# One four-tile MLP job split into two, under a new written order of all queues: two layers of banded attention and GELU MLP on one core

## The chip, the cores and the metric

The kernel runs on one core of a Trainium2 chip. The core has five engines with a queue each: TensorE (PE in the profile, its weight loads PEld), VectorE (DVE), ScalarE (ACT), GpSimd (POOL) and SyncE (SP), which here issues all DMAs. Every engine works through its own queue in the order in which the instructions were written, and waits on counters (semaphores) for the others. The metric is the device time of one execution in microseconds; less is better.

## The reference

Two layers, each an attention block (A) and an MLP block (B), both with a layer norm ahead and a residual sum behind. Both layers use the same weights. S = 2048 tokens, D = 512, 32 heads of 16, a causal band of W = 256 keys, F = 1792, all inputs bfloat16.

```python
def _A_ref(x, wqkv, wo):
    B, S, D = x.shape
    H = 32; Dh = D // H; W = 256
    q, k, v = ...                       # x @ wqkv, cut into heads
    scores = jnp.einsum("bhqd,bhkd->bhqk", q, k) * (Dh ** -0.5)
    mask = (idx[:, None] - idx[None, :] >= 0) & (idx[:, None] - idx[None, :] < W)
    scores = jnp.where(mask[None, None], scores, -1e9)
    p = _softmax(scores, axis=-1)
    o = jnp.einsum("bhqk,bhkd->bhqd", p, v)
    return (...)(o, 0, 2, 1, 3).reshape(B, S, D) @ wo

def _B_ref(x, w1, b1, w2, b2):
    h = jnp.einsum("bsd,df->bsf", x, w1) + b1
    h = _gelu(h)
    return jnp.einsum("bsf,fd->bsd", h, w2) + b2

x = A_x
x = x + _A_ref(_layernorm(x, axis=-1), A_wqkv, A_wo)
x = x + _B_ref(_layernorm(x, axis=-1), B_w1, B_b1, B_w2, B_b2)
x = x + _A_ref(_layernorm(x, axis=-1), A_wqkv, A_wo)
x = x + _B_ref(_layernorm(x, axis=-1), B_w1, B_b1, B_w2, B_b2)
```

## The kernel before

**Tiles and blocks.** The 2048 tokens are 16 tiles of 128. Over both layers they are counted on: tiles 0 to 15 are layer 1, 16 to 31 layer 2. An attention block b (0 to 15) is two tiles, 2b and 2b+1; blocks 0 to 7 are layer 1. X holds the running sum for all 16 tiles in on-chip memory.

**What one block does.** `lnq` (layer norm, transposed copy of the normed tile into xnTA by DMA, Q) and `kv` (K and V) come first. Then `attention(b)` goes through ten visits (five in blocks 0 and 8, where no keys lie behind). A visit is one set of score matmuls (L741), 512 score columns for each of four row groups, into four of the eight PSUM banks, then two exps on ScalarE (L748, two banks each) into the ring E, then masks (L769, VectorE or GpSimd). After five visits, and after ten, a PV (L793) multiplies E with V: 128 small matmuls (64 where no keys lie behind) that fill two banks; VectorE transposes (L802), inverts the sums (L806), scales (L810, VectorE or GpSimd) and transposes back (L816). Then come the output projection and the residual sum (L842) and the second layer norm, whose transposed tiles go to xnTB.

**MLP jobs.** `mlp(J)` (L846) handles the tiles of job J of the list JOBS (L457), an entry being (first tile, number of tiles). W1 (L857) makes 14 column groups of 128, four matmuls each, as wide as the job has tokens: 512 columns for four tiles, 256 for two. For the first six groups VectorE adds the bias (L865) and ScalarE applies the GELU to two groups at once (L868); for the other eight ScalarE does both (L873). W2 (L883) is 14 matmuls of 512 columns for each tile; GpSimd prepares X plus the second bias (L881), VectorE makes the sum (L885), and in layer 2 a DMA stores it. A job of even number reads xnTB half 0, of odd number half 1 (`js`), and a two-tile job uses the half J % 2 of gT.

**Exp and GELU.** ScalarE loads a table when it goes from exps to GELUs, and again on the way back (ACT_TABLE_LOAD in the profile).

**The order.** The functions put nodes into a plan (`_Plan.add`, L371); `run` (L391) then takes them in the order of the list `_ORDER`, gives the nodes named in `_ALT` to their second engine (evacuations L581/L583 VectorE or ScalarE; masks, L810 and part of the layer norm VectorE or GpSimd), and takes PSUM banks from `_BANKS`. `_PV_SEQ` is the order of the 32 groups of matmuls in a PV. `_Sched.op` records each node in its engine's queue with the waits that its tiles need. All plain projections and MLP matmuls are recorded by line L640 and are told apart by their tiles: W_sb with xnTB is W1, W_sb with gT is W2.

In ScalarE's queue, the GELUs of the job of tiles 4 to 7 stand after six exps of block 5, and those of tiles 8 to 11 after sixteen of block 7.

Of the kernel before, what the change touches and what calls it, by code (L numbers as in the profile page):

```python
# [19 lines left out]
class _Sched:  # L20
# [147 lines left out]
    33, 34, 0, 4, 7, 14, 17, 1, 13, 22, 18, 19, 56, 37, 36, 46, 35, 3, 26, 8, 41, 15, 27, 57, 60, 9, 61, 58, 39, 16,  # L168
    2, 59, 62, 20, 64, 28, 63, 10, 30, 24, 65, 11, 106, 104, 25, 47, 40, 67, 107, 105, 108, 38, 49, 54, 66, 32, 48,
    21, 68, 23, 31, 29, 69, 5, 80, 81, 82, 109, 55, 42, 110, 113, 111, 112, 114, 6, 83, 70, 71, 72, 73, 115, 126, 127,  # L170
    128, 129, 84, 74, 152, 130, 194, 195, 116, 117, 118, 119, 120, 97, 98, 99, 100, 150, 366, 85, 196, 101, 103, 368,
    86, 87, 88, 153, 151, 154, 75, 76, 77, 198, 367, 89, 155, 156, 200, 78, 12, 90, 91, 92, 93, 102, 79, 199, 131,
    132, 94, 157, 96, 95, 202, 204, 322, 121, 122, 123, 197, 133, 134, 203, 369, 124, 125, 136, 201, 137, 138, 205,
    158, 159, 216, 217, 143, 144, 145, 146, 135, 324, 139, 140, 212, 325, 323, 147, 218, 326, 327, 207, 519, 328, 208,
    209, 141, 329, 219, 214, 170, 171, 172, 173, 213, 370, 43, 160, 161, 162, 163, 174, 372, 371, 210, 520, 215, 374,
    164, 521, 148, 149, 175, 176, 376, 177, 178, 330, 375, 165, 166, 167, 206, 379, 179, 377, 381, 168, 380, 331, 44,
    142, 211, 220, 221, 180, 181, 182, 45, 183, 378, 169, 384, 385, 337, 222, 223, 373, 224, 338, 339, 340, 386, 394,
    395, 382, 388, 184, 186, 230, 231, 232, 233, 225, 226, 341, 383, 227, 396, 234, 237, 398, 228, 229, 400, 387, 389,
    238, 235, 185, 397, 236, 239, 399, 290, 402, 187, 188, 189, 190, 240, 390, 403, 241, 242, 243, 342, 343, 344, 522,
    345, 346, 407, 404, 405, 406, 191, 332, 333, 409, 334, 335, 336, 347, 348, 408, 412, 413, 414, 349, 350, 351, 244,  # L180
    50, 51, 192, 523, 524, 359, 360, 361, 362, 410, 527, 352, 353, 354, 355, 401, 356, 363, 563, 564, 245, 259, 525,
    260, 416, 357, 246, 261, 641, 252, 253, 565, 255, 275, 276, 277, 256, 254, 358, 411, 415, 257, 247, 258, 248, 249,
    262, 263, 264, 193, 528, 526, 284, 278, 364, 285, 250, 281, 269, 279, 280, 642, 282, 283, 270, 265, 391, 392, 417,
    639, 418, 640, 643, 271, 251, 393, 52, 53, 272, 644, 647, 266, 267, 273, 287, 365, 288, 286, 268, 645, 274, 307,
    308, 419, 420, 309, 310, 311, 312, 567, 544, 545, 546, 421, 547, 289, 306, 568, 313, 314, 315, 316, 571, 317, 569,
    529, 570, 530, 318, 646, 422, 531, 532, 572, 319, 320, 423, 548, 321, 573, 648, 575, 576, 533, 424, 425, 577, 427,
    428, 578, 429, 430, 539, 426, 487, 540, 541, 542, 431, 291, 581, 583, 543, 580, 434, 292, 293, 435, 582, 432, 294,
    295, 296, 574, 591, 592, 534, 535, 536, 537, 433, 593, 556, 538, 579, 557, 558, 898, 559, 896, 560, 436, 659, 660,
    561, 437, 297, 661, 662, 584, 595, 438, 439, 594, 298, 299, 300, 585, 649, 650, 651, 596, 566, 440, 652, 597, 663,
    586, 653, 599, 600, 549, 441, 587, 550, 301, 302, 303, 304, 305, 601, 602, 604, 551, 552, 605, 445, 446, 449, 450,  # L190
    606, 553, 447, 609, 562, 475, 476, 899, 897, 900, 472, 473, 610, 451, 459, 460, 456, 611, 452, 654, 461, 901, 904,
    453, 457, 607, 458, 902, 462, 442, 443, 655, 656, 454, 444, 469, 470, 598, 466, 471, 657, 658, 484, 485, 603, 664,
    665, 477, 448, 463, 608, 588, 474, 455, 481, 905, 482, 483, 464, 486, 612, 467, 468, 488, 489, 613, 589, 590, 465,
    478, 479, 490, 491, 614, 615, 480, 503, 683, 684, 492, 493, 666, 667, 616, 685, 494, 495, 687, 688, 668, 496, 497,
    498, 499, 686, 500, 501, 691, 617, 618, 669, 689, 690, 670, 671, 672, 693, 692, 502, 903, 916, 917, 918, 919, 694,
    673, 695, 675, 696, 698, 920, 624, 625, 626, 697, 699, 627, 504, 674, 628, 631, 701, 702, 619, 620, 621, 622, 623,
    505, 506, 555, 629, 630, 703, 711, 632, 507, 713, 508, 700, 509, 510, 511, 512, 633, 715, 906, 907, 704, 712, 908,
    716, 1018, 1019, 513, 514, 717, 705, 719, 721, 720, 1016, 634, 635, 637, 1017, 515, 909, 516, 517, 718, 638, 706,
    518, 724, 676, 714, 910, 1020, 707, 1021, 677, 678, 679, 723, 708, 726, 725, 729, 730, 680, 682, 926, 927, 928,
    933, 731, 636, 722, 934, 935, 728, 709, 710, 727, 936, 940, 929, 921, 922, 733, 923, 732, 941, 924, 925, 734, 937,  # L200
    938, 930, 939, 942, 944, 1024, 1022, 1023, 943, 946, 739, 740, 735, 948, 736, 911, 945, 912, 913, 737, 738, 914,
    950, 1025, 947, 741, 742, 949, 952, 915, 953, 955, 681, 951, 744, 743, 749, 745, 554, 746, 747, 748, 751, 954,
    958, 959, 750, 752, 1036, 1037, 1038, 957, 753, 754, 1039, 1040, 960, 968, 969, 757, 758, 1026, 970, 1027, 1028,
    1029, 755, 756, 962, 961, 972, 974, 1030, 973, 956, 976, 1275, 963, 977, 978, 971, 981, 975, 983, 964, 965, 966,
    786, 787, 788, 789, 982, 790, 986, 988, 1273, 781, 782, 979, 783, 932, 1274, 784, 785, 770, 771, 980, 987, 984,
    772, 1060, 985, 1062, 773, 990, 774, 764, 1061, 765, 766, 775, 767, 776, 777, 778, 1064, 1066, 768, 989, 991, 779,
    1065, 1068, 992, 817, 1063, 832, 818, 819, 1070, 802, 803, 1069, 1067, 807, 808, 827, 828, 829, 967, 996, 820,
    821, 993, 994, 759, 760, 761, 809, 810, 811, 848, 762, 1001, 1002, 997, 995, 998, 763, 999, 797, 798, 830, 1003,
    1004, 780, 1071, 1276, 1000, 1277, 769, 1278, 812, 813, 814, 791, 831, 822, 815, 816, 804, 805, 1005, 1008, 799,
    1009, 792, 823, 793, 794, 1395, 806, 795, 800, 1031, 796, 1006, 1279, 824, 825, 833, 864, 1007, 1393, 1032, 1072,  # L210
    1033, 1010, 1011, 834, 801, 1034, 1396, 826, 1035, 931, 849, 850, 835, 836, 1014, 1012, 837, 1281, 1073, 1074,
    851, 838, 852, 839, 840, 1075, 1076, 1078, 1079, 1080, 853, 841, 842, 854, 1015, 1041, 1042, 1043, 1044, 1045,
    1077, 855, 1082, 843, 844, 845, 1088, 1089, 856, 857, 1282, 858, 859, 860, 1081, 846, 861, 862, 847, 1092, 1090,
    865, 1091, 1093, 863, 1094, 881, 882, 1083, 1013, 1096, 883, 880, 866, 867, 1097, 1084, 868, 884, 1098, 1101,
    1103, 1099, 1085, 1086, 1087, 885, 886, 1102, 887, 888, 889, 890, 891, 1106, 869, 870, 871, 1095, 1394, 1397, 872,
    873, 1280, 1108, 1398, 1401, 1107, 1399, 1109, 1105, 892, 1317, 1319, 893, 874, 875, 876, 877, 1104, 894, 1318,
    1110, 1321, 1322, 1100, 878, 879, 1298, 1299, 1300, 895, 1301, 1302, 1293, 1294, 1323, 1295, 1296, 1325, 1111,
    1320, 1327, 1326, 1328, 1297, 1330, 1332, 1324, 1335, 1112, 1331, 1113, 1114, 1115, 1288, 1121, 1122, 1289, 1290,
    1337, 1291, 1292, 1225, 1334, 1336, 1345, 1123, 1329, 1124, 1116, 1125, 1128, 1338, 1347, 1117, 1118, 1119, 1346,
    1303, 1349, 1350, 1333, 1304, 1305, 1306, 1120, 1046, 1047, 1048, 1049, 1351, 1126, 1129, 1127, 1130, 1307, 1353,  # L220
    1354, 1131, 1309, 1134, 1283, 1135, 1284, 1355, 1285, 1132, 1133, 1286, 1358, 1339, 1340, 1050, 1287, 1360, 1359,
    1352, 1348, 1363, 1364, 1356, 1053, 1341, 1310, 1311, 1650, 1312, 1313, 1357, 1054, 1362, 1365, 1366, 1367, 1437,
    1439, 1055, 1056, 1136, 1137, 1314, 1400, 1138, 1361, 1139, 1342, 1368, 1051, 1057, 1059, 1058, 1438, 1140, 1402,
    1441, 1343, 1369, 1443, 1147, 1163, 1344, 1148, 1149, 1209, 1370, 1440, 1150, 1442, 1371, 1158, 1159, 1151, 1160,
# [189 lines left out]
def bass_interleave_layers__sliding_block__dense_activation_gelu__prompt_kernel(  # L414
# [39 lines left out]
    NWARM = 18  # L454
    PG = 2
    NPRE = 6
    JOBS = [(0, 2), (2, 2), (4, 4), (8, 4), (12, 4), (16, 4), (20, 4), (24, 4), (28, 2), (30, 2)]  # L457
    JLAG = 0
    W1_CUTS = ((0, 6), (6, 10), (10, 14))
    W2_CUTS = ((0, 4), (4, 8), (8, 11), (11, 14))  # L460
# [496 lines left out]
```

## Time and profile before

| what | value |
|---|---|
| median of 3 runs | 454.34 us (454.14 to 455.18) |
| the profiled execution | 452.28 us |
| its span on the core | 450.4 us |
| granted TensorE clock | 1.00 |
| busy TensorE, ScalarE, VectorE, GpSimd | 424.1, 388.0, 362.3, 204.1 us |
| exps L748 | 300, 1035 ns mean |
| GELUs L873 + L868, table loads | 80 + 30, and 18 of 1283 ns |
| last exp of block 3, 4, 5, 6, 7 ends at | 104.7, 126.4, 159.2, 181.3, 214.1 us |
| first W1 matmul to last X sum of job 2 (tiles 4 to 7) | 123.5 to 163.2 us |

The profile shows one execution. A group line names the source line, the engine, the operation and the tiles, the count, the busy time and the mean of one, and the idle time of the engine just before. A matmul's duration holds its way through the array, which overlaps the next matmul: eighteen matmuls of 512 columns that last 0.38 us each take 4.06 us together.

### The profile page before, as it was taken

How to read it: one execution, taken by the hardware profiler on the slowest of the kernel's cores; microseconds unless marked ns; L12 is line 12 of the kernel's file. 1: busy time of each engine (PE TensorE's matmuls, PEld its weight loads, DVE VectorE, ACT ScalarE, POOL GpSimd, SP SyncE). 2: the span in 40 equal slices, each digit the busy share in tenths (PEclk: the TensorE clock that was granted, in tenths of full speed). 3: DMA queues.
4: the chain of work that ended last, by engine and by line, in shares of the span. 5: the costliest groups of instructions: out<-in, count | busy, mean ns of one | idle time of the engine just before them, and what ended most of it. 6: DMA issues, size and time to landing. Idle time of an engine off the chain costs nothing.

```text
span 450.4 us, 16887 instructions
## 1 busy us (share of the span) xinstructions
PE 424.1 (94%) x7579; PEld 230.3 (51%) x7579; DVE 362.3 (80%) x650; ACT 388.0 (86%) x459; POOL 204.1 (45%) x219
## 2 busy tenths in 40 slices
PE   8979899997689988999999999999999999999997
PEld 4545656643444454455445444546555554544663
DVE  6999787989887689987899789877798768765852
ACT  3999898998889898899998998899897999899732
POOL 4476562453464445732284816653436143334320
PEclk9999999999999999999999999999999999999999
DMA  8684811112200201211022021010322013202000
GB/s 242 192 201 52 221 30 39 26 33 54 53 3 5 44 4 32 52 32 36 4 50 45 0 56 27 15 36 15 75 48 53 2 34 53 63 1 68 21 23 25
DMA packets 47972, 23.25 MB, mean 52 GB/s; under 512 B 33180, under 2 KB 47900, under 8 KB 47900
## 3 DMA queue, kind: packets, MB, share of 16 engines
q1 hardware_dynamic: 47900, 22.17, 21.4%
q8 instruction: 60, 0.98, 1.0%
q14 instruction: 12, 0.10, 0.1%
HBM read 8.00 MB, written 2.10 MB: 22 GB/s over the span
## 4 chain that ended last, share of the span: by engine, by line
PE 73%; DVE 20%; ACT 3%; DMA 2%; issue 1%; POOL 0%; DVEq 0%; SPq 0%
PE ps L640 57%; PE ps L793 8%; PE ps L741 7%; DVE E L769 4%; DVE OD L802 3%; ACT E L748 3%; DVE stat L592 2%; DVE Nb L810 2%; DVE KT L674 2%; DMA xnTB<-xn 2%; DVE xn L614 2%; DVE OT L816 1%; DVE X L885 1%; DVE X L842 1%; DVE Rc L806 1%
## 5 line engine op out<-in xcount | busy, mean ns | idle before, releaser
L748 ACT ACTIVATE E<-ps 128x1024 bf16<-128x1024 f32 x300 | 284.2, 1035 | 34.1 <-PE ps L741 33.1
L769 POOL TENSOR_TENSOR E<-E,mask 128x512 bf16<-128x512 bf16 (+2 forms) x111 | 123.3, 1122 | 144.0 <-ACT E L748 143.9
L640 PE MATMUL ps<-W_sb,gT 128*128 128x512 bf16 x448 | 116.2, 380 | 0.0
L640 PE MATMUL ps<-xnTB,W_sb 128*128 128x512 bf16 (+1 forms) x560 | 109.8, 337 | 2.1 <-DMA xnTB<-xn 1.4
L640 PEld LDWEIGHTS ps<-xnTB,W_sb 128*128 128x128 bf16 x560 | 51.9, 98 | 43.7 <-issue 4.1
L640 PE MATMUL ps<-xnTA,Wqkv_sb 128*128 128x256 bf16 x512 | 70.0, 273 | 4.1 <-DMA xnTA<-xn 2.2
L769 DVE TENSOR_TENSOR E<-E,mask 128x512 bf16<-128x512 bf16 (+2 forms) x125 | 63.7, 536 | 7.1 <-ACT E L748 7.0
L741 PE MATMUL ps<-QT,KT 32*128 32x128 bf16 (+3 forms) x1920 | 60.3, 231 | 7.8 <-ACT E L748 2.4
L640 PEld LDWEIGHTS ps<-W_sb,gT 128*128 128x128 bf16 x448 | 39.8, 98 | 41.5 <-issue 4.4
L640 PEld LDWEIGHTS ps<-xnTA,Wqkv_sb 128*128 128x128 bf16 x512 | 46.9, 98 | 24.2 <-issue 6.2
L741 PEld LDWEIGHTS ps<-QT,KT 32*128 32x128 bf16 x1920 | 28.3, 92 | 57.1 <-ACT E L748 34.5
L873 ACT ACTIVATE gT<-ps,b1T 128x512 bf16<-128x512 f32 (+1 forms) x80 | 43.6, 606 | 9.8 <-PE ps L640 9.5
L802 DVE STREAM_TRANSPOSE OD<-ps 128x1024 f32<-128x1024 f32 x32 | 39.9, 1248 | 14.4 <-PE ps L793 13.5
L881 POOL TENSOR_TENSOR Xb<-X,b2all 128x512 f32<-128x512 bf16 x32 | 38.4, 1206 | 25.2 <-DVE X L885 17.7
L865 DVE TENSOR_SCALAR gT<-ps,b1T 128x512 bf16<-128x512 f32 (+1 forms) x60 | 37.0, 633 | 10.7 <-PE ps L640 10.4
L793 PE MATMUL ps<-E,Va 64*17 64x64 bf16 (+3 forms) x1920 | 41.0, 230 | 4.8 <-DVE E L769 1.7
L592 DVE BATCH_NORM_STATS2 stat<-X 128x6 f32<-128x512 bf16 x64 | 43.3, 685 | 2.4 <-DMA X<-in_A_x_dram 1.7
L674 DVE TENSOR_TENSOR KT<-ps,parmask 128x1024 bf16<-128x1024 f32 x32 | 38.6, 1210 | 7.0 <-PE ps L640 6.8
L793 PE MATMUL ps<-E,Vs 64*17 64x192 bf16 (+3 forms) x1920 | 41.8, 230 | 0.1
L604 POOL TENSOR_TENSOR rstd<-rstd,mhalf 128x2 f32<-128x2 f32 (+1 forms) x33 | 23.7, 719 | 35.5 <-DVE rstd L598 30.3
L640 PE MATMUL ps<-Wo_sb,OT 128*128 128x512 bf16 x128 | 35.8, 381 | 2.0 <-DVE OT L816 1.8
L793 PEld LDWEIGHTS ps<-E,Va 64*17 64x17 bf16 x1920 | 29.3, 84 | 15.8 <-issue 8.3
(51 smaller groups left out, 356.6 us busy)
## 6 DMA issues: line engine op xcount, KB each, us to landing
Vs<-Va SPq DMA_DIRECT2D x64, 68.0 KB, 2.1
W_sb<-in_B_w_dram SPq DMA_DIRECT2D x4, 512.0 KB, 5.7
out_dram<-X SPq DMA_DIRECT2D x16, 128.0 KB, 2.5
X<-in_A_x_dram SPq DMA_DIRECT2D x3, 512.0 KB, 7.4
Wqkv_sb<-in_A_wqkv_dram SPq DMA_DIRECT2D x4, 256.0 KB, 4.4
W_sb<-in_B_w_dram SPq DMA_DIRECT2D x1, 768.0 KB, 5.6
W_sb<-in_B_w_dram SPq DMA_DIRECT2D x2, 384.0 KB, 4.8
Wqkv_sb<-in_A_wqkv_dram SPq DMA_DIRECT2D x1, 512.0 KB, 6.6
```

What stands on the lines that cost most here:

```text
L592: add("dve", lambda e, B, t=t, k6=k6: e.bn_stats(stat6[:, k6, :], X[:, t, :]), reads=["X%d" % t], writes=["st%d" % k6], key="bs%d" % (k + j))
L604: add("pool", lambda e, B, j=j, n=n: e.tensor_tensor(out=rstd[:, k + j : k + j + n], in0=rstd[:, k + j : k + j + n], in1=mhalf[:, 0:n], op ...
L640: r = e.matmul(ps[:, B[g][0], cols], lhsT, rhs, start=st, stop=sp)
L674: add("dve", lambda e, B, g=g, i=i: e.tensor_tensor(out=KT[:, kb, 2 * i : 2 * i + 2].rearrange("p c m a q -> p a (c m) q"), in0=ps[:, B[g] ...
L741: x = e.matmul(ps[:, bk[r], o : o + n], KT[rows, kb, c, m].rearrange("p a q -> p (a q)"), QT[rows, c, q : q + n], start=True, stop=True)
L748: add("act", lambda e, B, g_=g_, gi=gi: e.activation(E[:, 2 * gi : 2 * gi + 2, e0 : e0 + 512], ps[:, B[g_][0] : B[g_][0] + 2, :], AF.Exp, ...
L769: fn = lambda e, B: e.tensor_tensor(out=Ew, in0=Ew, in1=Mw, op=ALU.mult)
L793: x = e.matmul(ps[32 * r : 32 * r + VW, B[g][par], c % 2 * 2 * P + lo : c % 2 * 2 * P + hi], V[rows, (2 * b + m // 2) % VR, c * HC + 2 * r ...
L802: add("dve", lambda e, B: e.transpose(OD[:, s].rearrange("p a c q -> p (a c q)"), ps[:, B[g][0] : B[g][0] + 2, :]), reads=["ps:" + g], wri ...
L865: add("dve", lambda e, B, g=g, fc=fc: e.tensor_scalar(out=gT[:, fc, c0 : c0 + M], in0=ps[:, B[g][0], 0:M], scalar1=b1T[:, fc : fc + 1], sc ...
L873: add("act", lambda e, B, g=g, fc=fc: e.activation(gT[:, fc, c0 : c0 + M], ps[:, B[g][0], 0:M], AF.Gelu_apprx_tanh, bias=b1T[:, fc : fc + ...
L881: add("pool", lambda e, B, t=t, xs=xs: e.tensor_tensor(out=Xb[:, xs, :], in0=X[:, t, :], in1=b2all[:], op=ALU.add), reads=["X%d" % t, "b2a ...
```

## The change

The third entry of JOBS, tiles 4 to 7, becomes two entries. Everything that carries a job number behind it moves up by one: the old job 3 (tiles 8 to 11) is now job 4, and so on to job 10; so all later jobs read the other half of xnTB, and the two last jobs the other half of gT. The plan grows from 3080 to 3097 nodes: six more bias adds (L865), three more GELUs of two groups (L868) and eight more of one (L873). The 56 W1 nodes of the four-tile job, one matmul of 512 columns each, become 2 x 28 nodes of two matmuls of 256 columns.

All four lists are new. `_ALT` now gives 9 instead of 15 of the V copies to ScalarE, 13 instead of 12 of the Q copies, 3 instead of 4 of the transposed-tile copies; GpSimd has 113 instead of 111 masks and 15 instead of 12 of L810. In ScalarE's queue, the GELUs of tiles 4 and 5 stand after all exps of block 3, those of tiles 6 and 7 after all exps of block 4, those of tiles 8 to 11 after sixteen of block 7 as before. The source lines move down by two from the second list on.

```diff
@@ -165,198 +165,200 @@
 _ORDER = [
-    33, 34, 0, 4, 7, 14, 17, 1, 13, 22, 18, 19, 56, 37, 36, 46, 35, 3, 26, 8, 41, 15, 27, 57, 60, 9, 61, 58, 39, 16,
...
 _ALT = [
-    60, 62, 66, 69, 74, 108, 115, 125, 140, 154, 169, 191, 197, 205, 210, 215, 219, 239, 341, 363, 373, 377, 378, 383,
...
+    60, 66, 74, 101, 108, 115, 120, 125, 164, 197, 201, 210, 219, 223, 326, 336, 373, 378, 382, 388, 392, 401, 410,
...
 _PV_SEQ = [
-    (0, 2, 0), (1, 0, 0), (0, 0, 0), (1, 2, 0), (0, 3, 0), (1, 1, 0), (0, 0, 1), (1, 1, 1), (0, 1, 0), (1, 0, 1),
...
+    (1, 0, 0), (0, 3, 1), (0, -1, 0), (1, -2, 0), (0, 0, 1), (1, -4, 0), (1, 2, 1), (0, 0, 0), (1, 3, 1), (1, 3, 0),
...
 _BANKS = [
-    4, 5, 2, 1, 7, 5, 2, 0, 6, 2, 1, 4, 0, 6, 5, 4, 6, 2, 0, 1, 2, 4, 0, 7, 2, 4, 6, 0, 2, 6, 5, 6, 2, 4, 2, 0, 5, 4,
...
+    4, 7, 2, 6, 3, 7, 1, 2, 5, 6, 0, 3, 7, 2, 0, 4, 3, 6, 0, 4, 5, 6, 2, 4, 0, 6, 5, 6, 2, 0, 4, 2, 6, 0, 2, 4, 7, 6,
...
@@ -454,7 +456,7 @@
     NWARM = 18
     PG = 2
     NPRE = 6
-    JOBS = [(0, 2), (2, 2), (4, 4), (8, 4), (12, 4), (16, 4), (20, 4), (24, 4), (28, 2), (30, 2)]
+    JOBS = [(0, 2), (2, 2), (4, 2), (6, 2), (8, 4), (12, 4), (16, 4), (20, 4), (24, 4), (28, 2), (30, 2)]
     JLAG = 0
     W1_CUTS = ((0, 6), (6, 10), (10, 14))
```

## The prediction

> **What bounds the kernel now.** I read the page's busy table first, then the waits, then the busy time cut at the last exp (L748) of the attention blocks, then ScalarE's own timeline. A block, E0 to E15, is two tiles; E0 to E7 are layer 1.
>
> The page:
>
> ```profile
> PE 424.1 (94%) x7579; PEld 230.3 (51%) x7579; DVE 362.3 (80%) x650; ACT 388.0 (86%) x459; POOL 204.1 (45%) x219
> ```
>
> The waits (total us, times, longest):
>
> ```profile
> PEld ps L741 <- ACT E L748: 34.5, 79, 1.4
> ACT E L748 <- PE ps L741: 33.1, 50, 1.6
> ```
>
> TensorE and ScalarE are both near full, and in the waits they wait for each other by nearly the same sum (34.5 and 33.1 us): scores (L741) wait for exps to free banks, exps wait for scores. So the limit is to be looked for stage by stage.
>
> ```profile
> 104.70:126.40 21.70, 14.76 (x427) 8.66 (x427) 20.37 (x33) 18.83 (x23) 8.82 (x9) 1.00 0.26 53
> 126.40:159.20 32.80, 31.32 (x505) 15.25 (x503) 23.19 (x44) 29.28 (x35) 15.70 (x16) 1.00 0.09 18
> 159.20:181.30 22.10, 18.43 (x457) 9.88 (x455) 21.18 (x38) 19.73 (x23) 9.83 (x9) 1.00 0.09 18
> 181.30:214.10 32.80, 32.43 (x524) 17.06 (x523) 26.78 (x50) 30.56 (x36) 14.48 (x15) 1.00 0.20 41
> ...
> 222.50:249.20 26.70, 25.33 (x494) 12.77 (x493) 24.45 (x41) 23.86 (x28) 15.98 (x14) 1.00 0.19 40
> ```
>
> These are E4, E5, E6, E7 and E9 (columns: PE, PE weight loads, DVE, ACT, POOL busy, granted clock, DMA share, GB/s). E4 and E6 have no MLP in ScalarE's queue, and TensorE is short of work there (14.8 of 21.7 us, 18.4 of 22.1). E5 holds the whole job of tiles 4 to 7 and E7 the next one, and there TensorE is full. From E7 on it is nearly full to the end.
>
> ```profile
> 77.75 1.28 ACT L868 ACT_TABLE_LOAD   x1
> ...
> 83.65 1.28 ACT L748 ACT_TABLE_LOAD   x1
> 84.94 5.61 ACT L748 ACTIVATE E<-ps 128x1024 bf16<-128x1024 f32 x6
> ...
> 134.87 1.28 ACT L873 ACT_TABLE_LOAD   x1
> 136.16 1.32 ACT L873 ACTIVATE gT<-ps,b1T 128x512 bf16<-128x512 f32 x2
> ...
> 143.84 1.28 ACT L748 ACT_TABLE_LOAD   x1
> ```
>
> A job of two tiles holds ScalarE from the first table load to the next exp, 77.75 to 84.94: 7.19 us. The job of tiles 4 to 7 holds it from 134.87 to the end of the second load at 145.12: 10.25 us. Six exps in 5.61 us, the last lasting 1.035 us (L748's mean), make 0.915 us an exp.
>
> **The change on ScalarE.** Two jobs of two for one of four: 2 x 7.19 - 10.25 = +4.1 us, of which two more table loads are 2.6. The new choice of engines takes six Va copies off ScalarE (15 to 9) and one transposed-tile copy, and gives it one QT copy: six fewer at about 0.5 us of queue each (two Va copies take 1.13 us, of which the last 0.625), -3.0. Net about +1.1 us. By the Trainium skill (ScalarE: Activation LUTs, What ACT_TABLE_LOAD costs) a switch costs 1283 ns of load and 1380 ns of drain, 2.66 us, which speaks against the change. This trace agrees on the load, but shows exps starting 0.01 us after it and 1.31 us after the last gelu; by the page's figure, an estimate, ScalarE's sum would be 2.8 us higher.
>
> **On TensorE.** W1 (L857, recorded by L640) for these tiles: 56 matmuls of 512 columns become 112 of 256. 18 of 512 last 4.06 us, the last one 0.38, so 0.216 each; eight of 256 last 1.04, the last 0.273, so 0.110: 112 x 0.110 - 56 x 0.216 = +0.2 us. The 56 more weight loads (98 ns) lie under matmuls of 110; uncovered they would cost 5.5 us at most. W2 is the same 56 matmuls. Rows go between full-array, score and PV matmuls 324 times instead of 330.
>
> **On the others.** VectorE: bias adds (L865) 6 x 0.738 become 12 x 0.475, +1.3 us; six Va copies (0.672) come, three L810 (1.05) and two masks (0.48) go to GpSimd, one QT copy goes and one tile copy comes: about +1 us in all. GpSimd gets 3 x 1.07 + 2 x 1.17 = +5.6 at 45% busy. The DMAs are the same in number, in a new order on SP's queue; tiles 6 and 7 now use the other xnTB half, and all later jobs swap halves. TensorE's waits for xnTB are two, 1.4 us in all, so I take zero, with 1.4 either way.
>
> **Where it lies.** As all queues are new, I sum each stage's work in the written order, between last exps. TensorE: a unit is 512 columns at 0.216 us (one matmul of 512, two of 256, one visit of scores; a PV is five units, as 1.29 us less 0.22 for its last matmul); a change of shape is 0.13 us, since two full stages leave 0.12 (332.4 to 365.6: 33.2 us, 143 units, 23 changes, 30.9) and 0.12 (277.8 to 310.7: 32.9, 139, 23, 30.0), rounded up. ScalarE: exps at 0.91 plus the gelu intervals.
> E4: TensorE 52 units, 18 changes, 13.6 us; ScalarE 19 exps and two copies, 18.3. After: 102 units, 22 changes, 24.9; 21 exps and a job of two, 26.3.
> E5: 136 units, 22 changes, 32.2; 20 exps and the job of four, 28.5. After: 100, 21, 24.3; 19 exps and a job of two, 24.5.
> E6: 66, 18, 16.6; 21 exps, 19.1. After: 57, 18, 14.7; 22 exps and a copy, 20.5.
> E7: 132, 24, 31.6; 29.8. After: 112, 20, 26.8; 20 exps and a job of four, 28.5.
> The larger of the two, summed: 18.3 + 32.2 + 19.1 + 31.6 = 101.2 before, measured 109.4; after 26.3 + 24.5 + 20.5 + 28.5 = 99.8, so -1.4. What the stages took above it: where ScalarE leads 3.4 and 3.0, where TensorE leads 0.6 and 1.2. E9, where the two are close (23.7 and 22.7), took 3.0 above. After, none of the four is led by TensorE with room: 4 x 3.2 = 12.8 in place of 8.2, +4.6. So +3.2 if the excess goes with the class, -1.4 if each stage keeps its own; I take +3.2, since E9 is the row nearest to a stage where both are full.
> E0 to E3: the larger sums fall by 1.0 (copies off ScalarE); VectorE's work, summed from its rows' pitches, rises from 81.2 to 84.8 (bias adds and copies that stood later). Between -1.0 and +3.6 I take -0.5: VectorE is busy 25.8, 25.7 and 28.0 us in the three 30 us from 30 to 120, so there is room in two of them.
> E8 to the end, led by TensorE: 978 units are left after E7 instead of 966, with 168 changes both times: 12 x 0.216 = +2.6. In E9 TensorE leads after by 2.8 (24.6 against 21.8): the excess falls from 3.0 to about 0.9, -2.1; the other end is 0.
> Sum: 3.2 - 0.5 + 2.6 - 2.1 = +3.2; the ends are -1.9 and +9.4. The profiled execution took 452.28 us, span 450.4 and 1.9 around it: it becomes 455.5, span 453.6. The median shown is 454.34, 2.06 above it: 457.5.
>
> **The rivals.** *The interleaving pays (faster).* With MLP matmuls at hand in E4 and E5, TensorE has filler for every wait on a bank, and the stages keep the small excess: the low ends, -1.4 - 1.0 + 2.6 - 2.1 = -1.9, 452.4 us. For it: E4's idle 6.9 us of TensorE, and 17 us more matmul work (80 units) before E5's scores begin. Against it: total matmul work is the same, and ScalarE, the leader there, gets 4.1 us more. It decides if E4 to E7 take less than 109.4 us, the sum of the rest being near zero. The Trainium skill (Perfetto Trace Analysis, Optimization Strategy) says that where the most contended engine changes over time, interleaving the regimes may help; E4 and E5 are such a pair here, and that rule is this rival.
> *GpSimd's masks become late (slower).* Its work by stage, summed from its rows, goes from 7.5 to 18.3 us in E4, 14.4 to 19.0 in E10, 7.7 to 17.5 in E14. A mask (L769) takes 1.17 us there against 0.48 on VectorE, and one PV waited 1.7 us for one at 131.1. One such wait in each of the three stages: 3 x 1.7 = 5.1, 462.6 us. Against it: all waits of PV for GpSimd are 2.1 us now.
> *Nothing to measure.* The four stages give back half: 454 to 455 us.
> That the split is not made is excluded: the new instruction order holds 336 matmuls of 256 in W1 where there were 224.
>
> **How the numbers follow.** Forecast, 455.3 to 459.8 us: 0.38; late masks 0.16; interleaving 0.32; nothing 0.14. Three runs lie within 0.2%, so what lies within 0.2% can't be told from no change. Slower 0.54, same 0.14, faster 0.32. The range runs from below the low end (450.3) to the high end (463.7).
>
> **What would show it.** Right: 20 table loads; E4 and E5 near 29.5 and 27.7 us, E6 and E7 near 23.7 and 31.7; ScalarE idle before exps on scores about 3 us in each; TensorE full from E9. Wrong: E4 to E7 together under 109 us (interleaving), PV waits on L769 of POOL over 5 us (masks), or a first stretch to the end of E3 that differs from 104.7 by more than 2 us, since the whole order there is new and my sum gives it little.

## The result and the profile after

The changed kernel took 459.98 us (median of 4 runs, 458.74 to 460.16) beside 454.24 for the kernel before: 1.0144 times as long, interval 1.0108 to 1.0179. The profiled execution took 459.89 us against 452.28, its span 458.2 against 450.4: +7.8. All ratios are of fast executions; the one of run e9 (below) that was profiled was a slow one, 477.80 us beside 469.95 to 473.76, so its stages are a little long.

The page, busy time and the chain that ended last, after and then before:

```profile
PE 427.0 (93%) x7635; PEld 236.2 (52%) x7635; DVE 361.7 (79%) x657; ACT 390.7 (85%) x466; POOL 208.7 (46%) x224
...
PE 59%; ACT 17%; DVE 15%; DMA 4%; issue 2%; POOL 1%; SPq 1%; DVEq 0%
```

```profile
PE 73%; DVE 20%; ACT 3%; DMA 2%; issue 1%; POOL 0%; DVEq 0%; SPq 0%
```

On the chain TensorE's share falls and ScalarE's rises from 3% to 17%. TensorE has 56 more matmuls and 56 more weight loads and is busy 2.9 us longer, so 4.9 of the 7.8 us are idle time. Its waits with ScalarE (total us, times, longest) have hardly moved, 36.6 for 34.5 and 34.3 for 33.1:

```profile
PEld ps L743 <- ACT E L750: 36.6, 85, 1.4
...
ACT E L750 <- PE ps L743: 34.3, 56, 1.8
```

ScalarE's own timeline has the two small jobs as the forecast priced them (7.19 us each): from the first load to the end of the second 111.14 to 118.32, and 136.98 to 144.16.

```profile
111.14 1.28 ACT L870 ACT_TABLE_LOAD   x1
117.04 1.28 ACT L750 ACT_TABLE_LOAD   x1
136.98 1.28 ACT L875 ACT_TABLE_LOAD   x1
142.88 1.28 ACT L750 ACT_TABLE_LOAD   x1
```

The stages of after between last exps, in the columns of the forecast (PE, PE weight loads, DVE, ACT, POOL busy, granted clock, DMA share, GB/s): E2, E4, E5, E6, E7, E14, E15.

```profile
45.00:82.10 37.10, 33.11 (x571) 21.54 (x571) 33.92 (x66) 29.13 (x38) 13.89 (x15) 1.00 0.40 88
110.20:137.00 26.80, 26.23 (x520) 16.50 (x518) 23.28 (x44) 26.64 (x36) 16.31 (x18) 1.00 0.15 32
137.00:162.40 25.40, 24.05 (x497) 14.29 (x494) 21.21 (x41) 24.94 (x33) 10.33 (x13) 1.00 0.11 19
162.40:185.60 23.20, 16.15 (x431) 8.09 (x430) 20.09 (x39) 21.09 (x24) 11.89 (x10) 0.93 0.21 37
185.60:216.60 31.00, 29.09 (x505) 15.50 (x506) 23.39 (x40) 29.08 (x35) 14.96 (x16) 1.00 0.14 28
370.20:397.70 27.50, 25.81 (x488) 12.23 (x488) 18.18 (x33) 22.49 (x27) 16.71 (x16) 1.00 0.22 51
397.70:424.20 26.50, 26.50 (x454) 12.89 (x452) 15.68 (x29) 24.34 (x30) 12.71 (x13) 1.00 0.10 27
```

E2, E14 and E15 of before, which the forecast did not show:

```profile
44.90:77.70 32.80, 31.46 (x562) 20.70 (x561) 26.14 (x52) 28.41 (x38) 15.59 (x17) 1.00 0.41 99
365.60:388.20 22.60, 22.55 (x465) 11.16 (x463) 17.42 (x32) 21.75 (x25) 9.26 (x10) 1.00 0.28 55
388.20:417.90 29.70, 29.70 (x491) 13.82 (x490) 18.59 (x32) 27.33 (x32) 12.54 (x13) 1.00 0.14 38
```

Cut in three at the same marks:

| stretch | before | after | difference |
|---|---|---|---|
| start to the end of E3 | 104.7 | 110.2 | +5.5 (E2 alone +4.3) |
| E4 to E7 | 109.4 | 106.4 | -3.0 |
| behind E7, to the last sums of X | 233.4 | 238.6 | +5.2 (E12 to the end +5.0) |

"Last exp" needs a word of care, here and ahead of the forecast: the mark is the exp that the plan numbers last in its block, and in some blocks ScalarE's queue has one more exp of the block right behind it. Cut at the exp that really ends last, the three differences are +6.4, -3.9 and +5.2, E2's is +3.4 and E14's +5.8. So a single stage is known to about 1 us.

The four stages that the change is about are shorter, but they hold 371 units of TensorE's work where they held 386; 15 units at 0.216 are 3.2 us, which is as much as the gain. TensorE's idle time in them did not close, most of it moved: in E4 it was busy 14.8 of 21.7 us and is 26.2 of 26.8, while in E6 it falls from 18.4 of 22.1 to 16.2 of 23.2. And 10.7 us, of which some 3.2 are these deferred units, lie ahead of E4 and behind E7, where hardly any work of the split job stands.

### The profile page after: what moved, and what is told of

It reads as the page before. It is cut to its first block, busy times and chain, and to the rows that moved or that the text cites. A ratio compares the mean times of both kernels' runs of the same rounds, so it can differ in the third digit from the quotient of the medians.

```text
span 458.2 us, 17034 instructions
## 1 busy us (share of the span) xinstructions
PE 427.0 (93%) x7635; PEld 236.2 (52%) x7635; DVE 361.7 (79%) x657; ACT 390.7 (85%) x466; POOL 208.7 (46%) x224
## 3 DMA queue, kind: packets, MB, share of 16 engines
q1 hardware_dynamic: 47900, 22.17, 21.5%
## 4 chain that ended last, share of the span: by engine, by line
PE 59%; ACT 17%; DVE 15%; DMA 4%; issue 2%; POOL 1%; SPq 1%; DVEq 0%
PE ps L642 46%; ACT E L750 13%; PE ps L743 6%; PE ps L795 6%; DVE E L771 2%; DVE xn L616 2%; DMA Wqkv_sb<-in_A_wqkv_dram 2%; DVE KT L676 2%; DVE OD L804 2%; DVE gT L867 1%; DVE stat L594 1%; ACT gT L875 1%; DMA W_sb<-in_B_w_dram 1%; DVE QT L583 1%; DMA xnTB<-xn 1%
## 5 line engine op out<-in xcount | busy, mean ns | idle before, releaser
L750 ACT ACTIVATE E<-ps 128x1024 bf16<-128x1024 f32 x300 | 284.4, 1034 | 35.3 <-PE ps L743 34.3
L771 POOL TENSOR_TENSOR E<-E,mask 128x512 bf16<-128x512 bf16 (+2 forms) x113 | 125.3, 1124 | 119.3 <-ACT E L750 119.1
L642 PE MATMUL ps<-xnTB,W_sb 128*128 128x256 bf16 (+1 forms) x616 | 108.8, 321 | 2.3 <-DVE gT L867 1.3
L642 PEld LDWEIGHTS ps<-xnTB,W_sb 128*128 128x128 bf16 x616 | 58.0, 98 | 40.1 <-DVE gT L867 2.6
L642 PE MATMUL ps<-xnTA,Wqkv_sb 128*128 128x256 bf16 x512 | 71.5, 273 | 3.7 <-issue 1.4
L771 DVE TENSOR_TENSOR E<-E,mask 128x512 bf16<-128x512 bf16 (+2 forms) x123 | 62.1, 535 | 5.7 <-ACT E L750 5.7
L642 PEld LDWEIGHTS ps<-W_sb,gT 128*128 128x128 bf16 x448 | 39.5, 98 | 44.2 <-issue 5.8
L743 PEld LDWEIGHTS ps<-QT,KT 32*128 32x128 bf16 x1920 | 28.7, 93 | 60.6 <-ACT E L750 36.6
L642 PEld LDWEIGHTS ps<-xnTA,Wqkv_sb 128*128 128x128 bf16 x512 | 46.7, 98 | 24.9 <-issue 6.6
L875 ACT ACTIVATE gT<-ps,b1T 128x256 bf16<-128x256 f32 (+1 forms) x88 | 45.4, 573 | 12.3 <-PE ps L642 11.9
L867 DVE TENSOR_SCALAR gT<-ps,b1T 128x256 bf16<-128x256 f32 (+1 forms) x66 | 38.1, 595 | 14.0 <-PE ps L642 13.9
L795 PE MATMUL ps<-E,Vs 64*17 64x64 bf16 (+3 forms) x1920 | 41.9, 231 | 5.2 <-ACT E L750 1.9
L606 POOL TENSOR_TENSOR rstd<-rstd,mhalf 128x2 f32<-128x2 f32 (+1 forms) x33 | 24.9, 754 | 38.7 <-DVE rstd L600 37.7
L795 PEld LDWEIGHTS ps<-E,Vs 64*17 64x17 bf16 x1920 | 30.3, 84 | 14.8 <-issue 9.0
L642 PE MATMUL ps<-Wqkv_sb,xnTA 128*128 128x512 bf16 x128 | 34.8, 380 | 1.4 <-DVE KT L676 1.1
```

The source lines that it names most:

```text
L606: add("pool", lambda e, B, j=j, n=n: e.tensor_tensor(out=rstd[:, k + j : k + j + n], in0=rstd[:, k + j : k + j + n], in1=mhalf[:, 0:n], op ...
L642: r = e.matmul(ps[:, B[g][0], cols], lhsT, rhs, start=st, stop=sp)
L743: x = e.matmul(ps[:, bk[r], o : o + n], KT[rows, kb, c, m].rearrange("p a q -> p (a q)"), QT[rows, c, q : q + n], start=True, stop=True)
L750: add("act", lambda e, B, g_=g_, gi=gi: e.activation(E[:, 2 * gi : 2 * gi + 2, e0 : e0 + 512], ps[:, B[g_][0] : B[g_][0] + 2, :], AF.Exp, ...
L771: fn = lambda e, B: e.tensor_tensor(out=Ew, in0=Ew, in1=Mw, op=ALU.mult)
L795: x = e.matmul(ps[32 * r : 32 * r + VW, B[g][par], c % 2 * 2 * P + lo : c % 2 * 2 * P + hi], V[rows, (2 * b + m // 2) % VR, c * HC + 2 * r ...
```

## The experiments

A ratio is to the kernel before on the same chip; stages are in us, from one profiled execution.

### Orders spliced at a stage's end

Each takes queues, engines and banks from one kernel up to a mark (the last exp of a block) and from the other behind it; the order within a PV (`_PV_SEQ`) stays that of after in e1, e2 and e6 and that of before in e3 and e4. Theory A: each stretch's loss belongs to its own order and goes where that goes.

```diff
 # e1, tiles 4 to 7 in two jobs
-_ORDER, _ALT, _BANKS = after
+_ORDER, _ALT, _BANKS = before to the end of E3, then after
 # e2, in two jobs
+_ORDER, _ALT, _BANKS = after to the end of E7, then before
 # e3, in one job of four
+_ORDER, _ALT, _BANKS = after to the end of E3, then before
 # e4, in one job of four
+_ORDER, _ALT, _BANKS = before to the end of E7, then after
 # e6, in two jobs
+_ORDER, _ALT, _BANKS = after to the end of E11, then before
```

> The changed kernel, but the written order up to the last exp of block 3 is the one of before; from there on the new order, so the split job (tiles 4-5 and 6-7) and all that follows stay. Theory A (the loss is the new order's first stretch and last stretch, not the split): the first stretch cost 5.5 us in the trace and 4 units of matmul work (0.9 us) are owed, so about 455.4 us against 454.3 of before. Rival B (the split itself and what it adds on ScalarE costs it): stays within 1.5 us of 460.

> The changed kernel, but from the last exp of block 7 on the order of before. Theory A: the last stretch loses 5.2 us, of which 2.6 are matmul work that the new order had not done by then and that remains, so 2.6 us are won: about 457.4 us. Rival B: stays within 1.5 us of 460. Rival C (all of the loss is in the last stretch): about 454.8.

> The kernel before (one job of four tiles), but up to the last exp of block 3 the new order. Theory A: before plus 5.5 less 0.9 us, about 458.9 us, without any split. Rival B: like before, 454.3 within 1.

> The kernel before (one job of four tiles), but from the last exp of block 7 on the new order. Theory A: before plus 2.6 us, about 456.9, without any split. Rival B: like before, 454.3 within 1.

> The changed kernel, but from the last exp of the tenth visit of block 11 on the order of before; the two orders have nearly the same work behind them there (10 nodes apart, where the earlier cut at the end of block 7 had 29). Theory A: the new order's last stretch (block 13 on) loses 5.0 us against before, and at the cut 7 units of TensorE work (1.5 us) are owed: 3.5 us less than the changed kernel, about 1.0065 of before. Rival C (the last stretch is slow because of what comes into it, not by its own order): 1.0144 as the changed kernel.

| | time | ratio | E2 | E4 | E9 | E10 | E11 | E12 | E14 |
|---|---|---|---|---|---|---|---|---|---|
| before | | | 32.8 | 21.7 | 26.7 | 28.6 | 32.9 | 21.7 | 22.6 |
| after | 459.98 | 1.0144 (1.0108 to 1.0179) | 37.1 | 26.8 | 26.2 | 29.6 | 32.7 | 21.7 | 27.5 |
| e1 | 462.12 | 1.0214 (1.0179 to 1.0248) | 33.1 | 35.8 | 26.2 | 29.7 | 32.7 | 21.6 | 27.4 |
| e2 | 472.96 | 1.0445 (1.0400 to 1.0491) | 36.5 | 26.7 | 30.8 | 32.3 | 36.5 | 23.5 | 24.5 |
| e3 | 461.65 | 1.0190 (1.0152 to 1.0227) | 38.5 | 25.6 | 26.6 | 28.7 | 33.0 | 21.7 | 22.6 |
| e4 | 465.97 | 1.0313 (1.0266 to 1.0360) | 32.9 | 21.7 | 28.1 | 29.7 | 32.7 | 23.8 | 27.0 |
| e6 | 464.75 | 1.0289 (1.0248 to 1.0329) | 38.4 | 26.8 | 26.2 | 29.7 | 32.7 | 25.8 | 24.9 |

All five are slower than before, and none came out at a time that its expectation named; four are slower than after too, while e3's interval overlaps after's. So no sum over stretches gives their times, and theory A fails as an account of totals. It holds for two stages: E2 takes 33 us where the front is before's (e1, e4) and 36.5 to 38.5 where it is after's; E14 takes 27 with after's back and 23 to 25 with before's. A seam, the place where two orders meet, seems to cost some (e1's E4, e6's E12). But e2 could not be explained by a seam: behind E8 its order is that of before, and E9, E10 and E11 still take 4.1, 3.7 and 3.6 us more than there. Only the order within a PV is after's, and the next run takes that away.

### The split alone, and the place of an instruction in TensorE's stream

e5 keeps the order, engines, banks and PV order of before and only divides the job of tiles 4 to 7 where it stands; each table load serves both halves, so none is added.

```diff
-    JOBS = [(0, 2), (2, 2), (4, 4), (8, 4), ...]
+    JOBS = [(0, 2), (2, 2), (4, 2), (6, 2), (8, 4), ...]
 # each of the old job's nodes replaced, in its place, by the two of the new jobs
```

> The order of before, with the job of tiles 4 to 7 split where it stands: at each place of a W1 group, bias add or GELU of the four-tile job stand those of tiles 4-5 and then of 6-7, in one GELU interval with no further table loads. It costs two banks for one at each W1 group and eleven more GELU instructions (2 x 7.19 less two loads of 1.28 each against 10.25 less the same: +1.6 us on ScalarE, +0.2 on TensorE). Theory A (the halved width is nearly free, the new order costs the time): before plus 0 to 2 us. Rival B (the halved instructions themselves cost): before plus 4 to 7 us.

It took 480.63 us, 1.0583 (1.0512 to 1.0653): 28 us slower than before and 20 slower than after, where its two theories had 0 to 2 and 4 to 7. Again E9 to E11 took 29.2, 32.5 and 36.3 us, 9.8 more than before's, with the same order on every engine there. In the waits of e5, matmuls of scores and PVs stood (were idle) for 16.6 us, 8.0 and 8.6, for nothing that the profile shows ("issue"). What else moved is TensorE's stream of instructions: it has 112 more ahead of E8. The page of before shows how that stream arrives (queue, kind: packets, MB, share):

```profile
q8 instruction: 60, 0.98, 1.0%
```

7579 matmuls, 7579 weight loads and the 157 other instructions recorded for TensorE's own queue make 15,315 in 60 pieces, 255 each. A PV issues 256 instructions in about 1.2 us; a four-tile W1 group issues eight in 0.9. Theory F: TensorE stands where a piece is used up faster than the next one comes. The next runs leave order and work alone and only shift the stream. In e9, e14, e13 (before) and e11 (after) the 18 matmuls on zeros that run while the first loads are under way are cut into more pieces of fewer columns; in e10 (the split in place) and e12 (after) 18 of the 28 W1 groups of tiles 4 to 7 are made in two halves.

```diff
 # e9: 56 matmuls more; e14: 16; e13: 128; e11, on after: 64
-add("pe", lambda e, B, bk=h % 8: e.matmul(ps[:, bk, :], gT[:, 0, 0:P], gT[:, 0, :], start=True, stop=True),
+add("pe", lambda e, B, bk=h % 8, h=h: warm(e, bk, 56 * (h + 1) // NWARM - 56 * h // NWARM + 1),
 # warm(e, bk, k): the same 512 columns in k matmuls
 # e10, on e5, and e12, on after: 72 matmuls more
+if J in (2, 3) and 18 * (14 * (J - 2) + fc + 1) // 28 > 18 * (14 * (J - 2) + fc) // 28:
+    pe_group(g, [(W1_sb[:, dc, fc * P : (fc + 1) * P], xnTB[:, js, dc, h0 : h0 + P], slice(h0, h0 + P), dc == 0, dc == DC - 1)
+                 for h0 in (0, P) for dc in range(DC)], 4, ...)
+    return g
```

> The kernel before, plan and orders untouched; 56 of TensorE's matmuls on zeros ahead of the first load's arrival are cut in pieces, so that 56 matmuls with their weight loads (112 instructions) more are issued there, with the same columns in all, and every later instruction stands 112 places further on in TensorE's stream, as far as the split moves what is behind it. Theory F (TensorE's instructions come in pieces of 256, and it stands for 1.3 to 2.4 us where such a piece has to come within a fast stretch): the places of the fetches move against the work, the idle time near fetches rises from 7.5 us to over 15, and the time from 452.3-454.3 to 459-482, the stages of E9 to E15 going up as they did in the split in place. Rival G (the fetches are harmless; the re-cut orders lose by the order itself): 452 to 455.

> The split in place in the order of before (480.6 as it stood), with 18 of the 28 first-product groups of the two small jobs done in two halves of 128 columns, which makes 72 matmuls and 72 weight loads more within E4 to E7: with the 112 of the split, 256 instructions, one whole piece, so that all behind E7 stands as in the kernel before to a piece. Columns in all are the same. Theory F: E9 to E15 take again what they take in before, 252 us together from the end of E8, each stage within 0.7 us, and the time falls to 456-468. Rival G: it stays at 478-483.

> The kernel after, untouched but for 64 matmuls more (128 instructions, half a piece) in the pieces that the matmuls on zeros at the start are cut into. Theory F: the time leaves 458.7-460.2 by 2 us or more, to either side, 452 to 480; idle time near fetches leaves 7.8 us by 2 or more. Rival G: 458 to 460.5.

> The kernel after with 18 of the 28 first-product groups of its two small jobs in two halves, so that from E8 on the instructions' numbers differ from those of before by a whole piece. Theory F: E2 (37.1 us) stays, since nothing ahead of it is changed; E8 to E15 and the end change by 1 us or more in some stage with a fetch gap appearing or going there; 454 to 470. Rival G: all stages within 0.5 us of after's, 458.5 to 461.

> The kernel before with 128 matmuls more at the start in place of e9's 56, cut from the same matmuls on zeros: 256 instructions, one whole piece, so that every later instruction stands at its old place within a piece. Theory F (what counts is where an instruction stands within a piece of 256): 451.5 to 455, within 0.5% of the kernel before, with stages as there. Rival H (the more numerous matmuls at the start cost by themselves, through the clock or the start of the stages): 473 or more, at least the 21 us that 56 cost.

> The kernel before with 16 matmuls more at the start (32 instructions, an eighth of a piece). Theory F, with the gaps being set by whether a fetch falls within a fast stretch of some 250 instructions: a few of the fetches change sides, 451 to 460. If every place counts: 460 or more. Rival H (cost by number of matmuls): 458, that is 16/56 of e9's 21 us.

| on | instructions more | time | ratio | E4 | E5 | E9 | E10 | E11 |
|---|---|---|---|---|---|---|---|---|
| before, e13 | 256 at the start | 453.17 | 1.0006 (0.9973 to 1.0039) | 21.6 | 33.0 | 26.6 | 28.7 | 32.9 |
| before, e14 | 32 at the start | 464.32 | 1.0230 (1.0185 to 1.0275) | 26.8 | 33.4 | 26.7 | 28.7 | 34.7 |
| before, e9 | 112 at the start | 473.17 | 1.0427 (1.0364 to 1.0489) | 19.1 | 35.6 | 29.2 | 32.9 | 36.9 |
| split, e5 | 112 by the split | 480.63 | 1.0583 (1.0512 to 1.0653) | 22.9 | 39.9 | 29.2 | 32.5 | 36.3 |
| split, e10 | 112 and 144, by E7 | 460.10 | 1.0156 (1.0090 to 1.0222) | 23.5 | 39.5 | 26.7 | 28.7 | 32.9 |
| after, e11 | 128 at the start | 461.64 | 1.0200 (1.0150 to 1.0250) | 28.3 | 26.2 | 27.3 | 29.7 | 32.7 |
| after, e12 | 144 by E7 | 469.36 | 1.0371 (1.0322 to 1.0421) | 29.3 | 29.5 | 27.8 | 31.3 | 32.8 |

This settles it for the order of before. There 256 instructions more cost nothing, 112 cost 20 us and 32 cost 10, so neither their number nor the work counts, only the place within a piece. In e10, one whole piece further on, all stages behind E7 are those of before to 0.1 us, and 20.5 of e5's 28 us are gone. On after the answer is less sharp: e12 lost 9.4 us, as theory F allowed, but e11's 461.64 is 1.7 us from after, where F asked for 2 or more and G for at most 460.5.

What it looks like: TensorE's waits of e9 and of e13 (source lines stand six lower than in before: L747 is scores, L799 PV, L646 the plain matmuls); in before, matmuls wait 0.2 us in all on "issue":

```profile
PE ps L799 <- issue: 10.5, 6, 2.3
...
PE ps L747 <- issue: 9.3, 7, 2.4
...
PE ps L646 <- issue: 7.3, 39, 0.6
```

```profile
PE ps L646 <- issue: 5.5, 34, 0.3
```

The 5.5 us of e13 are the cut matmuls at the start; the 19.8 us of e9's PVs and scores are gone. One of them, the PV of E9 in e9's timeline (start, us, then the idle time before) and the same PV in before's:

```profile
249.14 0.42 PE L799 MATMUL ps<-E,Va 64*17 64x128 bf16 x4
249.35 0.24 PE L799 MATMUL ps<-E,Vs 64*17 64x128 bf16 x7
251.83 0.19 PE L799 MATMUL ps<-E,Vs 64*17 64x64 bf16 x1 [2.24 <-issue]
251.96 0.40 PE L747 MATMUL ps<-QT,KT 32*128 32x192 bf16 x12
```

```profile
240.71 0.42 PE L793 MATMUL ps<-E,Va 64*17 64x128 bf16 x4
240.92 0.25 PE L793 MATMUL ps<-E,Vs 64*17 64x128 bf16 x8
241.10 0.40 PE L741 MATMUL ps<-QT,KT 32*128 32x192 bf16 x12
```

With the last matmul of the PV left, the array stands for 2.24 us; a packet of the instruction queue is on its way from 249.6. In e14 the same falls into a score visit, and the clock pays too: six W1 matmuls of 512 columns take 2.74 us, where five at 0.216 and a last one of 0.38 make 1.46.

```profile
126.65 0.34 PE L747 MATMUL ps<-QT,KT 32*128 32x192 bf16 x7
129.14 0.44 PE L747 MATMUL ps<-QT,KT 32*128 32x192 bf16 x5 [2.16 <-issue]
...
131.88 2.74 PE L646 MATMUL ps<-xnTB,W_sb 128*128 128x512 bf16 x6
```

The Trainium skill (Runtime: NRT & Kernel Launch, Instruction fetch mechanics) has the refill in blocks of 256 instructions, as e13 bears out, and calls the cost of crossing a block "mostly hidden". Most of the 60 are hidden here; in e9 thirteen stands in PVs and scores cost 19.8 us, up to 2.4 each.

### Why E2 of after is longer

```diff
 # e7: the copies of V of tiles 5 to 9 on ScalarE
+_ALT: nodes 191, 356, 363, 553, 560 added
 # e8: W2 pieces 2 and 3 (nodes 52, 53) right behind 0 and 1 on SP
-_ORDER = [..., 50, 51, ..., 528, ..., 526, 52, 53, ...]
+_ORDER = [..., 50, 51, 52, 53, ..., 528, ..., 526, ...]
 # e15: five masks and one L812 of E2 on GpSimd; e16: e15 and e8
+_ALT: nodes 405, 420, 570, 575, 579, 580 added
 # e17: after, e18: before, 37 steps up to the end of E2 on the other kernel's engine
-_ALT
+_ALT
```

> The changed kernel with five V copies of layer 1 (tiles 5 to 9) on ScalarE instead of VectorE, nothing else. Theory D (VectorE is the limit in block 2's stretch, 33.9 us busy of 37.1, and the score matmuls wait 2.4 us for V copies behind its masks): 2 to 4 us less than the changed kernel, 1.006 to 1.010 of before. Rival E (that stretch is late for the W2 load): no change, 1.0144.

> The changed kernel with the two last pieces of the W2 load issued right after the two first ones on SP's queue (before three V shifts and two transposes), nothing else. Rival E (block 2's stretch is late for the W2 load, 5.5 us of DMA on the chain): 2 to 4 us less than the changed kernel. Theory D: at most the 1.1 us that TensorE waits for the load.

> The kernel after in its own order, with five masks and one normalisation of the stage E2 on GpSimd (14 of 37 us busy there) in place of VectorE; TensorE's instructions are untouched. Theory D (E2 is bound by VectorE, 34 of 37.1 us busy): VectorE loses 4 to 5 us there, E2 falls to 33.5-35.5, the time to 455-458. Rival W (E2 waits for the W2 pieces and for its own order on TensorE): E2 stays at 36.5-37.5, the time at 458.5-460.5.

> The edit of e15 together with the W2 pieces 2 and 3 right behind 0 and 1 on SP (that alone took E2 to 36.3 and the time to 458.7). Theory D: as e15 and up to 1 us less, 454 to 457.5. Rival W: E2 36 to 36.5, 458 to 459.5. If both hold it back: E2 at 33 or less, 453 to 456.

> The kernel after in its own order, but up to the end of E2 each step with two possible engines is on the engine that before uses (37 steps change: copies, masks, normalisations, small sums). Theory D (the engines are what E1 and E2 lose): the end of E2 falls from 82.1 us to 77.5-79.5 and the time to 454.5-457. Rival O (the order of the steps loses it): the end of E2 at 81 to 83.5, the time 458 to 461.

> The kernel before in its own order and with the same 37 steps on the engines that after uses. Theory D: the end of E2 rises from 77.7 us to 80.5-83, the time by 3 to 5 us, to 455.5-458.5. Rival O: the end of E2 at 77 to 79, the time 452 to 454.5.

| | time | ratio | E1 | E2 | end of E2 |
|---|---|---|---|---|---|
| before | | | 22.1 | 32.8 | 77.7 |
| after | 459.98 | 1.0144 | 22.5 | 37.1 | 82.1 |
| e7 | 458.71 | 1.0144 (1.0102 to 1.0187) | 23.1 | 38.2 | 82.7 |
| e8 | 458.70 | 1.0131 (1.0095 to 1.0168) | 21.9 | 36.3 | 79.8 |
| e15 | 458.71 | 1.0114 (1.0074 to 1.0154) | 22.7 | 38.1 | 82.2 |
| e16 | 459.34 | 1.0135 (1.0092 to 1.0179) | 21.9 | 37.7 | 80.8 |
| e17 | 468.40 | 1.0349 (1.0310 to 1.0387) | 27.3 | 44.5 | 95.3 |
| e18 | 461.09 | 1.0210 (1.0157 to 1.0263) | 28.0 | 34.3 | 85.8 |

No single cause held. The late W2 pieces are what two of E2's waits name, and with them early E2 is 0.8 us shorter; in e7, e15 and e16 it is 0.6 to 1.1 longer. But none of these differences can be told from the spread: e2, e3 and e6 have after's front untouched, and their E2 takes 36.5, 38.5 and 38.4 us in the one execution profiled of each. Fetches don't explain the 33 us of before's front: half a piece on (e11) after's E2 still takes 36.2 us. The waits of TensorE in E2 of after:

```profile
PE ps L743 <- DVE Va L583: 2.4, 2, 2.1
...
PE ps L642 <- DMA W_sb<-in_B_w_dram: 1.1, 2, 0.9
```

e7 changed the engine waited for: with ScalarE copying V, TensorE stood once for exps (L706 there), at 56.9 us:

```profile
PE ps L699 <- ACT E L706: 3.1, 1, 3.1
```

e15 was a weaker test of VectorE than its expectation supposed. Six steps left VectorE, but its busy time in E2 fell only from 33.92 to 33.05 us:

```profile
44.10:82.20 38.10, 33.01 (x567) 21.55 (x571) 33.05 (x60) 29.36 (x38) 19.89 (x21) 1.00 0.34 86
```

The steps that stayed became longer: a mask of 512 columns on VectorE takes 1044 ns on the mean there, 664 in E2 of after and 476 in E2 of before. After's own timeline shows how a step can become so long: an xn of 0.37 us takes 1.28 when it starts with a mask of GpSimd.

```profile
55.43 0.37 DVE L616 TENSOR_SCALAR xn<-X,statmv,rstd 128x512 bf16<-128x512 bf16 x1
...
61.92 1.28 DVE L616 TENSOR_SCALAR xn<-X,statmv,rstd 128x512 bf16<-128x512 bf16 x1 [0.39 <-POOL rstd L606]
```

```profile
61.91 1.15 POOL L771 TENSOR_TENSOR E<-E,mask 128x512 bf16<-128x512 bf16 x1
```

GpSimd's mask ends at 63.06, the xn at 63.20. The Trainium skill (SBUF — State Buffer, Terms) has a port pair that the two engines take by turns for a whole instruction; these rows agree with it. So a step moved to GpSimd is partly paid for on VectorE.

e17 and e18 missed both theories: each order is 8 to 9 us slower on the other's engines. Engines and order seem fitted to each other, and what E2 loses can't be put down to one of them. That part stays open.

## Why the prediction was wrong

The direction was right, the size about half: +3.2 forecast, +5.7 between the medians (+6.5 by the ratio), +7.6 between the two profiled executions. That the direction came right is luck in part: of the forecast's three stretches the front was off by +6.0 us, E4 to E7 by -6.2 and the back by +4.7.

**The front, taken at -0.5 us, is the step that failed.** It took +5.5, beyond its upper end of +3.6, by the bound that the forecast itself had named (E3's end 2 us off 104.7). The reason given, that VectorE had room in two of three 30 us, was read off before's queues, which the change replaces. In E2 of after VectorE is busy 33.9 of 37.1 us, in before 26.1 of 32.8: statistics that stood in E1, two xn that stood in E3 and nine steps that before gives to GpSimd or ScalarE came together there. That it is nearly full is shown; that this alone sets the stage is not (e7, e15), so why the front takes longer stays open.

**E4 to E7, +3.2 forecast, came out at -3.0, and with the 15 deferred units at about +0.2.** So the rival "interleaving pays" met its own test (106.4, under 109.4), while its total did not come. The end of -1.4 that the forecast gave for stages that keep their own excess was the nearer one. The larger sums were right for E4 and E5: 26.3 and 24.5 forecast, 26.8 and 25.4 measured, only 0.5 and 0.9 above them. The excess by class (3.2 us for every stage that TensorE doesn't lead) was wrong there: these two stages, in which both are busy with their own work, had no such excess. It came in E6 and E7, 2.7 and 2.5 us. E6 holds a stand of 1.81 us on issue within a PV, and behind it 3.4 us at half clock: 23.2 us at 0.93 lose 1.6. In e11, which has neither, E6 takes 21.5 us, 1.0 above the sum.

```profile
169.80 0.25 PE L795 MATMUL ps<-E,Vs 64*17 64x64 bf16 x10 [1.81 <-issue]
```

**Behind E7, +0.5 forecast (2.6 less 2.1), measured +5.2.** The 12 units came. E9's excess fell by 1.4 us and not by 2.1: it took 26.2 with work of 24.6, before 26.7 with 23.7. From E12 on, which the forecast took to be full by work alone, TensorE is idle 2.8 us for 0.3 before. E14 is 4.9 us longer and E15 3.2 shorter, since work stands earlier; what E14 loses is mostly one wait, of scores for VectorE's sum of X, which before does not have:

```profile
PE ps L743 <- DVE X L887: 1.8, 1, 1.8
```

The same wait of 1.8 us is there in e1, e4, e11 and e12, which have after's order throughout the back, at three places within a piece; E14 takes 27.0 to 27.5 us in all of them. So it belongs to the order and not to the stream. About 1.4 of the 5.2 us are not placed.

**What was priced rightly:** the two jobs on ScalarE (7.18 us each for 7.19, 20 table loads in all), the switch of tables at 1.31 us, W1 by units. **GpSimd's masks** did not become late: the matmuls of PV waited for L771 on GpSimd once, 1.0 us, under the 5 that the rival needed.

**What the forecast had no term for** is the stream: 112 instructions more, costed as cover for weight loads, shift everything behind them by seven sixteenths of a piece. In the order of before that is worth 20 us (e9, e5 against e10), six times the forecast. After pays little of it: its scores and PVs stand on issue for 1.8 us in all, those of before 0.2, of e5 16.6. Neither shift of its stream that was tried made it faster (e11, whose interval overlaps after's, and e12), so it stands at a good place, whether by choice or by chance. The split in the old order costs 28 us, with the stream put right behind E7 7.9 (e10: E4 +1.8, E5 +6.7), and in the new order 5.7. What of these 7.9 is the split itself is not shown, since e10's E4 ran at a granted clock of 0.85 and its E5 at 0.96 (23.5 us at 0.85 lose 3.5, 39.5 at 0.96 lose 1.6), and before's at 1.00. No version tried beats the kernel before; e13 equals it.

## What to carry to other kernels

When an edit adds or removes instructions of an engine that issues hundreds in a microsecond, test it twice: as it is, and with cheap instructions added ahead of it to make up a whole piece (256 here); the difference between the two is the fetch and not the edit. An order written for one stream and one choice of engines can't be cut and joined, nor its stages costed by sums alone: the sums were a floor here (E4 and E5 came within 0.9 us of them, E6 and E7 2.7 and 2.5 above), and the stages with the least change in the diff can carry the loss. Work moved from VectorE to GpSimd was not all gone from VectorE (e15).

## What the hardware showed that was not expected

- Thirty-two more instructions at the start of TensorE's stream made a kernel 2.3% slower, 256 more made no difference (0.9973 to 1.0039).
- Stands of TensorE of about 2 us are sometimes followed by half the clock for 3.4 us, or twice that. In e9 this happened behind three of the seven stands of 1.9 us or more, and once behind two shorter ones; e14 has two such dips of 6.8 us, before none ahead of its end.
- An xn on VectorE lasted 3.5 times as long beside a mask of GpSimd (1.28 for 0.37 us).
